# Splitting of weights moved from GpSimd to VectorE, every second cast of attention weights moved to ScalarE, sums of token tiles moved to VectorE

## The chip, the cores and the metric

The kernel runs on one core of a Trainium2 chip. The metric is the device time of one execution in microseconds; of several runs the median is taken. Engines are named as in the profile: PE (TensorE), DVE (VectorE), ACT (ScalarE), POOL (GpSimd), and SP, whose queue issues most DMAs.

## What is computed

An attention without softmax, followed by two MLPs on its 6016 tokens (two batches of 3008):

```python
# u, v: (2, 3008, 256); z: (2, 3008, 64); w_in: (256, 2048); w_out: (2048, 256)
attn = np.maximum((z @ z.T) / 3008, 0.0) ** 2      # per batch
x = (u * (attn @ v)).reshape(6016, 256)
h = x @ w1_in;  x = np.maximum(0.01 * h, h) @ w1_out
h = x @ w2_in;  x = (s * np.maximum(h, 0.0) ** 2 + b) @ w2_out
```

## The kernel before

All matrix products run on operands that are split in two: `hi` is the value cast to the matmul's type (fp32r), `lo` is the value minus `hi`. A product is then three matmuls: hi x hi, hi x lo, lo x hi. Wherever the text says "split" it means one cast for `hi` and one subtraction for `lo`.

**Attention** runs over 12 tiles of queries (512 wide; 448 for the last of each batch), and within a tile over 12 units (`UA`) of two key blocks, 144 units or steps in all. In a unit `scores` (L296) makes four matmuls (L303) into a PSUM tile `f`, ACT applies Relu (L306) and Square (L307) into `a`, DVE casts `hi` (L308) and subtracts `lo` (L314; for the last unit of a tile, L310 and L312). `queue_values` (L317) queues 12 matmuls (L329; 10 in the last unit of a tile) which PE takes two units later, behind the scores of that unit. The first of them reads `hi`, the second `lo`. Every engine works through its own instructions in the order in which the program issues them.

**Weights.** While attention runs, the MLPs' weights, which arrive as 64-bit numbers, are narrowed to 32 bits, split, and written to DRAM. There are 32 items of 512 columns: for each MLP `m`, four groups `g`, kinds `in` and `out`, two halves `h`. An item starts every third step (`s0`), except around the change of batch. `narrow` (L138) spreads its pieces over steps: three on DVE at s0, s0+1, s0+2 (L149; L154, L157; L162, L165), the last of which is followed by `join` on POOL (L178 for `out`; L186 and L190 to L193 for `in`). `halve` (L195) makes the split at s0+5: for `out` items the cast on ACT (L207) and the subtraction on POOL (L208), in the second MLP after a running sum on POOL (L203); for the second half of an `in` item, two casts on ACT (L213) and two subtractions on POOL (L214), for the seven blocks of weights that one step of the MLPs needs. `store` issues the DMAs at s0+8.

Around the change of batch (steps 60 to 74) the keys and values of the second batch are split, with the subtractions on POOL (L116, L252).

**MLPs.** Token tiles are taken in six pairs, and the first product of each MLP is done with seven products of blocks instead of eight (a scheme of Strassen's kind), so each pair needs sums of its token tiles: `pair_sums` (L362) makes four differences T1 to T4 on POOL (L369), and `pair_split` splits them. A pair has eight quads (q = 0 to 7). A quad makes seven products (L395), four sums on DVE from PSUM (L618, L640, L641, L652, L654), activates the previous quad's result on ACT, splits it (`spread`, L586: `hi` on ACT in the first MLP and on DVE in the second, L593; `lo` on DVE, L594) and queues the second product's matmuls (L414), of which PE takes eight after each third of the quad. The sums of the next pair are issued from q = 4 on, one in each third of a quad. At q = 4 of the second pair of the first MLP `bias_columns` (L448) adds two halves on DVE (L449) for a small matmul on PE (L452).

The order of all this is written out by hand: `at(step, fn)` puts a piece of work in front of a unit.

Of the kernel before, what the change touches and what calls it, by code (L numbers as in the profile page):

```python
# [10 lines left out]
F32 = mybir.dt.float32  # L11
F32R = mybir.dt.float32r
# [3 lines left out]
ALU = mybir.AluOpType  # L16
P = 128
# [11 lines left out]
def relu2_attention__then__leaky_mlp__then__relu2_mlp_kernel(  # L29
# [25 lines left out]
    nc = tc.nc  # L55
# [19 lines left out]
    pairs = sorted((ts[i], ts[i + 1]) for ts in by_width.values() for i in range(0, len(ts), 2))  # L75
# [47 lines left out]
    wt_of, staged = {}, {}  # L123
# [14 lines left out]
    def narrow(item):  # L138

        words = raws[item].rearrange("p (n w) -> p n w", w=2)
        low, high = words[:, :, 0], words[:, :, 1]
        w = single.tile([P, 2 * D], F32, tag="w", name="w_single", bufs=4)
        bits = w.bitcast(I32)

        def one():
            nc.vector.tensor_scalar(  # L149
                out=low, in0=low.bitcast(U32), scalar1=2.0 ** -29, scalar2=None, op0=ALU.mult  # L150
            )

        def two():
            nc.vector.tensor_scalar(  # L154
                out=bits, in0=high, scalar1=0x7FFFFFFF, scalar2=None, op0=ALU.bitwise_and
            )
            nc.vector.tensor_scalar(  # L157
                out=w, in0=w, scalar1=HIGH_MAX, scalar2=HIGH_MIN, op0=ALU.min, op1=ALU.max
            )

        def three():
            nc.vector.tensor_scalar(  # L162
                out=bits, in0=bits, scalar1=3, scalar2=0x3FFFFFFF, op0=ALU.logical_shift_left, op1=ALU.bitwise_and
            )
            nc.vector.scalar_tensor_tensor(  # L165
                out=bits, in0=high, scalar=-(1 << 30), in1=bits, op0=ALU.bitwise_and, op1=ALU.bitwise_or
            )
            join(item, w, low)

        return [(0, one), (1, two), (2, three), (5, lambda: halve(item, w)), (8, lambda: store(item))]  # L170

    def join(item, w, low):
        m, g, kind, h = item
# [19 lines left out]
        add(out=a[S4], in0=a[A12], in1=a[S2], op=ALU.subtract)  # L193

    def halve(item, w):  # L195
        m, g, kind, h = item
        add = nc.gpsimd.tensor_tensor
        if kind == "out":
            if m == 2:
                if g == 0 and h == 0:  # L200
                    nc.gpsimd.tensor_copy(out=wsum, in_=w)
                else:
                    add(out=wsum, in0=wsum, in1=w, op=ALU.add)  # L203
            if h == 0:
                staged[m, g, kind] = [outw.tile([P, 2, 2, 2 * D], F32R, tag="outw", name="stage_o")]
            t = staged[m, g, kind][0]
            nc.scalar.copy(out=t[:, h, 0, :], in_=w)  # L207
            add(out=t[:, h, 1, :], in0=w, in1=t[:, h, 0, :].bitcast(F32), op=ALU.subtract)  # L208
        elif h == 1:
            wt = wt_of.pop((m, g))  # L210
            staged[m, g, kind] = [outw.tile([P, 2, 7, P], F32R, tag="outw", name="stage_i") for _ in range(2)]
            for q, t in enumerate(staged[m, g, kind]):
                nc.scalar.copy(out=t[:, 0], in_=wt[:, q, 0:7, :])  # L213
                add(out=t[:, 1], in0=wt[:, q, 0:7, :], in1=t[:, 0].bitcast(F32), op=ALU.subtract)  # L214

    def store(item):
        m, g, kind, h = item
# [78 lines left out]
    def scores(t, p):  # L296
        bb, c, n = tiles[t]
        f = ps_f.tile([P, 2, QT], F32, tag="f", name="f")
        for j in range(2):
            kb = 2 * p + j  # L300
            lhsT = zk[bb, kb // 4][:, (kb % 4) * P:(kb % 4 + 1) * P]
            for h in range(2):
                nc.tensor.matmul(f[:, j, :n], lhsT=lhsT, rhs=zq[t][:, h, :n], start=h == 0, stop=h == 1)  # L303
        a = work.tile([P, 2, QT], F32, tag="a", name="a")[:, :, :n]
        hi, lo = split_parts(a, n)
        nc.scalar.activation(out=a, in_=f[:, :, :n], func=AF.Relu, scale=scale)  # L306
        nc.scalar.activation(out=a, in_=a, func=AF.Square)  # L307
        nc.vector.tensor_copy(out=hi, in_=a)  # L308
        if p == UA - 1:
            nc.vector.tensor_sub(out=lo[:, 0], in0=a[:, 0], in1=hi[:, 0].bitcast(F32))  # L310
            h1 = hi[HALF:P, 1]
            nc.vector.tensor_sub(out=h1, in0=a[HALF:P, 1], in1=h1.bitcast(F32))  # L312
        else:
            nc.vector.tensor_sub(out=lo, in0=a, in1=hi.bitcast(F32))  # L314
        return hi, lo
# [43 lines left out]
            xin[m, t] = xio.tile([P, 2, QT], F32, tag="xin", name="x_in")  # L359
            nc.sync.dma_start(out=xin[m, t][:, :, :n], in_=x_d[m, t][:, :, :n])  # L360

    def pair_sums(m, pr):  # L362

        n = tiles[pr[0]][2]
        (b11, b21), (b12, b22) = ([xin[m, t][:, k, :n] for k in range(2)] for t in pr)
        new = {k: tpool.tile([P, QT], F32, tag="tsum", name="tsum", bufs=4)[:, :n] for k in ("T1", "T2", "T3", "T4")}

        def sub(out, x, y):
            return lambda: nc.gpsimd.tensor_tensor(out=out, in0=x, in1=y, op=ALU.subtract)  # L369

        tsum[m, pr] = {**new, "B11": b11, "B21": b21, "B22": b22}
        return [
            sub(new["T1"], b12, b11), sub(new["T2"], b22, new["T1"]),
            sub(new["T3"], b22, b12), sub(new["T4"], b21, new["T2"]),
        ]
# [81 lines left out]
    def at(step, fn):  # L457
        hooks.setdefault(max(step, 0), []).append(fn)

    with tc.manual_schedule():  # L460
# [61 lines left out]
        for item, s0 in zip(items, places):  # L522
# [2 lines left out]
                    at(s0 + later, piece)  # L525
            at(s0 - 5, lambda item=item: load_w(item))
            hooks.setdefault(s0, []).insert(0, go)
        done = places[len(items) - 1] + 9
        assert done < n_att - 12

        def open_pairs():
# [3 lines left out]
        at(done, open_pairs)  # L535
        at(done + 1, lambda: load_pair(1, pairs[0]))
        sums = []
        at(done + 5, lambda: sums.extend(pair_sums(1, pairs[0])))
        for i in range(4):
            at(done + 5 + i, lambda: sums.pop(0)())  # L540
        for i, name in enumerate(ORDER):
# [61 lines left out]
        for m, pr, q in quads:  # L603
            n = tiles[pr[0]][2]
            k = pair_of.index((m, pr))
            ahead = pair_of[k + 1] if k + 1 < len(pair_of) else None
            x = [ps_x.tile([P, QT], F32, tag="x", name=f"x{i}") for i in range(3)]
            x1, x2, x3 = (y[:, :n] for y in x)
            w = work.tile([P, 2, QT], F32, tag="a", name="a")
            s1, u2 = (w[:, i, :n] for i in range(2))  # L610
            cs = [cpool.tile([P, 2, QT], F32, tag="c", name="c")[:, :, :n] for _ in range(2)]
            c11, c21, c12, c22 = cs[0][:, 0], cs[0][:, 1], cs[1][:, 0], cs[1][:, 1]

            product(x[0], m, pr, q, A11, "B11", True)
            nc.scalar.copy(out=s1, in_=x1)  # L615
            product(x[1], m, pr, q, S2, "T2", True)
            product(x[2], m, pr, q, S1, "T1", True)
            nc.vector.tensor_tensor(out=u2, in0=x2, in1=s1, op=ALU.add)  # L618

            if q == 0 and k:  # L620
                pair_split(m, pr, ORDER[5:7], nc.vector)
            if q == 1 and ahead:
                load_pair(*ahead)
            if q == 6 and ahead:
                pair_split(*ahead, ORDER[0:2], nc.vector)
            if q == NQ - 1 and ahead:
                pair_split(*ahead, ORDER[2:3], nc.vector)
            activate(0)
            if before and before[0] == 1:
                activate(1)  # L630
            if q == 4 and ahead:
                sums.extend(pair_sums(*ahead))
            if sums:
                sums.pop(0)()
            step_chunk()

            product(x[0], m, pr, q, A12, "B21", False)
            act_of(m, c11, x1)
            product(x[1], m, pr, q, S3, "T3", False)
            nc.vector.tensor_tensor(out=c22, in0=x2, in1=s1, op=ALU.add)  # L640
            nc.vector.tensor_tensor(out=c22, in0=x3, in1=c22, op=ALU.add)  # L641
            spread(0)
            if before and before[0] == 2:
                activate(1)
            if q == NQ - 1 and ahead:
                pair_split(*ahead, ORDER[3:4], nc.vector)
            if sums:
                sums.pop(0)()
            step_chunk()

            product(x[1], m, pr, q, A22, "T4", False)
            nc.vector.tensor_tensor(out=c21, in0=x2, in1=s1, op=ALU.add)  # L652
            product(x[2], m, pr, q, S4, "B22", False)
            nc.vector.tensor_tensor(out=c12, in0=x3, in1=u2, op=ALU.add)  # L654
            spread(1)
            if q == NQ - 1 and ahead:
                pair_split(*ahead, ORDER[4:5], nc.vector)
            if sums:
                sums.pop(0)()
            if m == 1 and pr == pairs[-1]:  # L660
                fetch_in(2, q)
            step_chunk()
            before = (m, pr, q, cs)
            if m == 1 and pr == pairs[1] and q == 4:
                bias_columns()
# [40 lines left out]
```

## Time and profile before

| | |
|---|---|
| time, three runs | 1541.13, 1545.22, 1546.81 us; median 1545.22 |
| the profiled execution | 1542.53 us; its span 1540.8 us |
| busy: PE | 1508.7 us (98%) |
| busy: DVE | 1151.4 us (75%); in the first third 90% or more of most slices |
| busy: ACT | 843.7 us (55%) |
| busy: POOL | 333.5 us (22%), mostly in the first third |
| mean granted clock of PE | 0.996 |

Attention takes the first 545 us, the first MLP until about 1027, the second the rest. Busy shares are averages over these stages. Since PE works nearly all the time, its short waits, and what ends them, carry the reading.

### The profile page before, as it was taken

To read this page: it belongs to the slowest core of one execution; us is meant where nothing else is said; L and a number is where in the kernel's file an instruction comes from. 1 tells how busy PE (TensorE), PEld (TensorE's weight loads), DVE (VectorE), ACT (ScalarE), POOL (GpSimd) and SP (SyncE) were. 2 spreads that over 40 slices of the span, in tenths; PEclk is the share of its full clock that TensorE was granted. 3 is DMA by queue.
4 is the path that set the end of the run, shared out by engine and by line. 5 is a ranking of instruction groups with operands and counts; after the bars stand their busy time and mean duration, and the time that the engine had idled before them with its cause. 6 is when DMAs were issued, how large, how long until landed. Compare 5 with 4: busy or idle time off the path is not lost.

```text
span 1540.8 us, 17008 instructions
## 1 busy us (share of the span) xinstructions
PE 1508.7 (98%) x6604; PEld 1239.7 (80%) x6604; DVE 1151.4 (75%) x1365; ACT 843.7 (55%) x1046; POOL 333.5 (22%) x212
## 2 busy tenths in 40 slices
PE   8999999999999999999999999999999999999998
PEld 6877778777787888888889888887877778877786
DVE  7999987999998756656565656566776777676766
ACT  6656666665665644545454546454545545454543
POOL 0344546456654410101010100110010101010000
PEclk9999999999999999999999999999999999999999
DMA  5243433432345430101010101341010101010000
GB/s 156 90 142 110 152 136 115 136 130 84 135 151 217 151 133 1 55 1 51 1 55 1 52 1 65 137 154 55 1 56 1 52 1 55 0 52 1 28 0 28
DMA packets 38834, 113.25 MB, mean 74 GB/s; under 512 B 4064, under 2 KB 13792, under 8 KB 36704
## 3 DMA queue, kind: packets, MB, share of 16 engines
q1 hardware_dynamic: 38528, 111.88, 21.2%
q8 instruction: 52, 0.85, 0.2%
q10 hardware_dynamic: 160, 0.26, 0.1%
q14 instruction: 30, 0.25, 0.1%
q0 software_dynamic: 64, 0.00, 0.0%
HBM read 70.58 MB, written 41.55 MB: 73 GB/s over the span
## 4 chain that ended last, share of the span: by engine, by line
PE 82%; DVE 12%; issue 4%; ACT 1%; DMA 0%; SPq 0%; DVEq 0%
PE acc L414 33%; PE x L395 29%; PE acc L329 16%; PE f L303 5%; DVE lo L314 3%; DVE hi L308 3%; DVE w_single L162 1%; DVE lo L594 1%; DVE hi L312 1%; ACT a L307 1%; ACT a L306 1%; DVE w_single L154 1%; DVE lo L310 1%; DMA raw_v<-in_v_dram 0%; DVE raw_w L149 0%
## 5 line engine op out<-in xcount | busy, mean ns | idle before, releaser
L395 PE MATMUL x<-top,stat_i 128*128 128x512 f32 (+1 forms) x2016 | 498.6, 386 | 0.8 <-DVE c L640 0.8
L414 PE MATMUL acc<-hi,stat_o 128*128 128x512 f32 (+1 forms) x1536 | 483.8, 386 | 0.0
L395 PEld LDWEIGHTS x<-top,stat_i 128*128 128x128 f32 x2016 | 378.2, 188 | 74.4 <-DVE c L640 1.2
L329 PE MATMUL acc<-hi,stat_v 128*128 128x512 f32 (+1 forms) x1152 | 377.2, 392 | 0.4 <-DVE hi L312 0.4
L414 PEld LDWEIGHTS acc<-hi,stat_o 128*128 128x128 f32 x1536 | 288.4, 188 | 54.0 <-DVE hi L593 0.5
L414 PE MATMUL acc<-lo,stat_o 128*128 128x512 f32 (+1 forms) x768 | 302.1, 393 | 3.7 <-DVE lo L594 3.6
L329 PEld LDWEIGHTS acc<-hi,stat_v 128*128 128x128 f32 x1152 | 219.1, 190 | 45.1 <-DVE hi L308 2.1
L306 ACT ACTIVATE a<-f 128x1024 f32<-128x1024 f32 (+1 forms) x144 | 145.5, 1011 | 185.2 <-PE f L303 150.6
L640 DVE TENSOR_TENSOR c<-x,a 128x512 f32<-128x512 f32 (+1 forms) x96 | 65.3, 681 | 234.7 <-PE x L395 234.7
L594 DVE TENSOR_TENSOR lo<-c,hi 128x1024 fp32r<-128x1024 f32 (+1 forms) x192 | 237.9, 1239 | 3.3
L329 PE MATMUL acc<-lo,stat_v 128*128 128x512 f32 (+1 forms) x552 | 217.2, 393 | 14.3 <-DVE lo L314 14.3
L615 ACT COPY a<-x 128x512 f32<-128x512 f32 (+1 forms) x96 | 55.6, 579 | 312.7 <-PE x L395 312.7
L314 DVE TENSOR_TENSOR lo<-a,hi 128x1024 fp32r<-128x1024 f32 (+1 forms) x132 | 209.9, 1590 | 4.6
L369 POOL TENSOR_TENSOR tsum<-x_in 128x512 f32<-128x512 f32 (+1 forms) x24 | 39.5, 1644 | 772.2 <-DMA x_in<-x_d 685.4
L414 PEld LDWEIGHTS acc<-lo,stat_o 128*128 128x128 f32 x768 | 144.1, 188 | 49.5 <-DVE lo L594 23.6
L303 PE MATMUL f<-zq,zk 128*128 128x512 f32 (+1 forms) x576 | 157.0, 395 | 7.2 <-DVE zk L252 5.4
L307 ACT ACTIVATE a<-a 128x1024 f32<-128x1024 f32 (+1 forms) x144 | 150.4, 1044 | 4.6
L308 DVE CAST hi<-a 128x1024 fp32r<-128x1024 f32 (+1 forms) x144 | 117.0, 813 | 39.4 <-ACT a L307 38.8
L329 PEld LDWEIGHTS acc<-lo,stat_v 128*128 128x128 f32 x552 | 105.0, 190 | 40.2 <-DVE lo L314 20.0
L303 PEld LDWEIGHTS f<-zq,zk 128*128 128x128 f32 x576 | 109.9, 191 | 31.4 <-ACT zq L265 5.4
L618 DVE TENSOR_TENSOR a<-x,a 128x512 f32<-128x512 f32 (+1 forms) x96 | 65.2, 680 | 73.7 <-PE x L395 72.9
L584 ACT ACTIVATE c<-c 128x1024 f32<-128x1024 f32 (+1 forms) x96 | 100.3, 1045 | 3.1
(62 smaller groups left out, 1229.9 us busy)
## 6 DMA issues: line engine op xcount, KB each, us to landing
in_d<-stage_i SPq DMA_DIRECT2D x16, 896.0 KB, 8.0
stat_i<-in_d SPq DMA_DIRECT2D x16, 896.0 KB, 4.8
x_in<-x_d SPq DMA_DIRECT2D x20, 512.0 KB, 4.6
raw_w<-in_w_in_dram SPq DMA_DIRECT2D x16, 512.0 KB, 4.6
raw_w<-in_w_out_dram SPq DMA_DIRECT2D x16, 512.0 KB, 4.4
out_d<-stage_o SPq DMA_DIRECT2D x8, 1024.0 KB, 6.4
stat_o<-out_d SPq DMA_DIRECT2D x8, 1024.0 KB, 6.5
raw_v<-in_v_dram SPq DMA_DIRECT2D x14, 384.0 KB, 3.7
```

The lines of the kernel that those rows point to most:

```text
L303: nc.tensor.matmul(f[:, j, :n], lhsT=lhsT, rhs=zq[t][:, h, :n], start=h == 0, stop=h == 1)
L306: nc.scalar.activation(out=a, in_=f[:, :, :n], func=AF.Relu, scale=scale)
L307: nc.scalar.activation(out=a, in_=a, func=AF.Square)
L308: nc.vector.tensor_copy(out=hi, in_=a)
L314: nc.vector.tensor_sub(out=lo, in0=a, in1=hi.bitcast(F32))
L329: nc.tensor.matmul(acc_t[t][dh][:, :n], lhsT=w[:, wh, o:o + P], rhs=x[:, blk % 2, :n], start=blk == 0 and i == 0, stop=half and i == n_i - 1,)
L395: nc.tensor.matmul(x[:, :n], lhsT=w[:, wh, left, :], rhs=r[:, xh, :n], start=first and i == 0, stop=i == 2, skip_group_check=not first,)
L414: nc.tensor.matmul(acc[dh][:, :n], lhsT=w[:, q % 2, wh, o:o + P], rhs=x[:, f, :n], start=q == 0 and f == 0 and i == 0, stop=last,)
L584: nc.scalar.activation(out=c, in_=c, func=AF.Square)
L594: nc.vector.tensor_sub(out=lo, in0=c, in1=hi.bitcast(F32))
L618: nc.vector.tensor_tensor(out=u2, in0=x2, in1=s1, op=ALU.add)
L640: nc.vector.tensor_tensor(out=c22, in0=x2, in1=s1, op=ALU.add)
```

## The change

In `narrow`, `halve` becomes a list of pieces that stand at steps of their own: for `out` items the cast on ACT at s0+4 and the subtraction at s0+5; for the second half of `in` items the first cast at s0+6, the first subtraction and the second cast at s0+7, the second subtraction at s0+8. The subtractions go from POOL to DVE. The running sum of L203 stays on POOL. `store` moves from s0+8 to s0+10, and what comes after the last item moves one step. In `scores`, the cast of `hi` goes from DVE to ACT in units with odd `p`. In the MLPs `pair_sums` issues on DVE; the first pair's sums, which run during attention, stay on POOL.

```diff
@@ narrow
-        return [(0, one), (1, two), (2, three), (5, lambda: halve(item, w)), (8, lambda: store(item))]
+        return [
+            (0, one), (1, two), (2, three),
+            *(((4 if item[2] == "out" else 6) + i, fn) for i, fn in enumerate(halve(item, w))),
+            (10, lambda: store(item)),
+        ]
@@ halve
+        if kind == "in" and h == 0:
+            return []
+
+        def hi_out():
             if m == 2:
                 if g == 0 and h == 0:
                     nc.gpsimd.tensor_copy(out=wsum, in_=w)
                 else:
-                    add(out=wsum, in0=wsum, in1=w, op=ALU.add)
+                    nc.gpsimd.tensor_tensor(out=wsum, in0=wsum, in1=w, op=ALU.add)
             if h == 0:
                 staged[m, g, kind] = [outw.tile([P, 2, 2, 2 * D], F32R, tag="outw", name="stage_o")]
+            nc.scalar.copy(out=staged[m, g, kind][0][:, h, 0, :], in_=w)
+
+        def lo_out():
             t = staged[m, g, kind][0]
-            nc.scalar.copy(out=t[:, h, 0, :], in_=w)
-            add(out=t[:, h, 1, :], in0=w, in1=t[:, h, 0, :].bitcast(F32), op=ALU.subtract)
-        elif h == 1:
-            wt = wt_of.pop((m, g))
-            staged[m, g, kind] = [outw.tile([P, 2, 7, P], F32R, tag="outw", name="stage_i") for _ in range(2)]
-            for q, t in enumerate(staged[m, g, kind]):
-                nc.scalar.copy(out=t[:, 0], in_=wt[:, q, 0:7, :])
-                add(out=t[:, 1], in0=wt[:, q, 0:7, :], in1=t[:, 0].bitcast(F32), op=ALU.subtract)
+            nc.vector.tensor_tensor(out=t[:, h, 1, :], in0=w, in1=t[:, h, 0, :].bitcast(F32), op=ALU.subtract)
+
+        def hi_in(q):
+            t = outw.tile([P, 2, 7, P], F32R, tag="outw", name="stage_i")
+            staged.setdefault((m, g, kind), []).append(t)
+            nc.scalar.copy(out=t[:, 0], in_=wt_of[m, g][:, q, 0:7, :])
+
+        def lo_in(q):
+            t = staged[m, g, kind][q]
+            nc.vector.tensor_tensor(
+                out=t[:, 1], in0=wt_of[m, g][:, q, 0:7, :], in1=t[:, 0].bitcast(F32), op=ALU.subtract
+            )
+            if q == 1:
+                wt_of.pop((m, g))
+
+        if kind == "out":
+            return [hi_out, lo_out]
+        return [lambda: hi_in(0), lambda: (lo_in(0), hi_in(1)), lambda: lo_in(1)]
@@ scores
-        nc.vector.tensor_copy(out=hi, in_=a)
+        (nc.scalar.copy if p % 2 else nc.vector.tensor_copy)(out=hi, in_=a)
@@ pair_sums
-            return lambda: nc.gpsimd.tensor_tensor(out=out, in0=x, in1=y, op=ALU.subtract)
+            return lambda: eng.tensor_tensor(out=out, in0=x, in1=y, op=ALU.subtract)
@@ before attention
-        done = places[len(items) - 1] + 9
+        done = places[len(items) - 1] + 10
-        at(done + 5, lambda: sums.extend(pair_sums(1, pairs[0])))
+        at(done + 5, lambda: sums.extend(pair_sums(1, pairs[0], nc.gpsimd)))
@@ the quads
-                sums.extend(pair_sums(*ahead))
+                sums.extend(pair_sums(*ahead, nc.vector))
```

## Rows read from the trace of the kernel before

**Rows 1.** Order of time, PE: score matmuls opening units 3, 12, 60, 84, 132 (start, us).
```profile
18.28 1.09 PE L303 MATMUL f<-zq,zk 128*128 128x512 f32 x4
...
51.22 1.09 PE L303 MATMUL f<-zq,zk 128*128 128x512 f32 x4
...
232.10 0.97 PE L303 MATMUL f<-zq,zk 128*128 128x448 f32 x4
...
317.64 1.09 PE L303 MATMUL f<-zq,zk 128*128 128x512 f32 x4
...
505.43 0.97 PE L303 MATMUL f<-zq,zk 128*128 128x448 f32 x4
```

**Rows 2.** Waits, whole run: who waited for whom, us in total, times, longest.
```profile
PEld acc L414 <- DVE lo L594: 23.6, 53, 2.0
...
PEld acc L329 <- DVE lo L314: 20.0, 16, 2.0
...
PEld f L452 <- DVE wtot L449: 0.9, 1, 0.9
```

**Rows 3.** Order of time, POOL and DVE around the stall at unit 20.
```profile
73.67 5.34 POOL L214 TENSOR_TENSOR stage_i<-wt,stage_i 128x896 fp32r<-128x896 f32 x2 [1.06 <-ACT stage_i L213]
...
74.67 2.36 DVE L162 TENSOR_SCALAR w_single<-w_single 128x512 int32<-128x512 int32 x1
```

**Rows 4.** Lines L162, L165, L308, L178, L203: count, then shortest, median, longest in ns.
```profile
L162 DVE TENSOR_SCALAR w_single<-w_single x32: 411/421/2361, 53.0 to 476.8; 128x512 int32<-128x512 int32 x32
...
L165 DVE SCALAR_TENSOR_TENSOR w_single<-raw_w,w_single x32: 691/693/2499, 53.5 to 477.2; 128x512 int32<-128x512 int32 x32
...
L308 DVE CAST hi<-a x144: 612/686/2272, 12.2 to 544.7; 128x1024 fp32r<-128x1024 f32 x120, 128x896 fp32r<-128x896 f32 x24
...
L178 POOL TENSOR_TENSOR w_single<-w_single,raw_w x16: 1666/1689/1702, 79.6 to 478.0; 128x512 int32<-128x512 int32 x16
...
L203 POOL TENSOR_TENSOR wsum<-wsum,w_single x7: 2142/2157/2160, 337.3 to 479.8; 128x512 f32<-128x512 f32 x7
```

**Rows 5.** Busy by stretch: PE, PEld, DVE, ACT, POOL, then PEclk, DMA share, GB/s.
```profile
328.00:331.00 3.00, 3.00 (x8) 2.35 (x8) 2.96 (x5) 2.40 (x3) 0.68 (x2) 0.50 0.00 0
```

**Rows 6.** Groups by line and shape: busy us, mean ns, idle time before them.
```profile
L640 DVE TENSOR_TENSOR c<-x,a 128x512 f32<-128x512 f32 x80 | 55.3, 692 | 199.7 <-PE x L395 199.7
...
L594 DVE TENSOR_TENSOR lo<-c,hi 128x896 fp32r<-128x896 f32 x32 | 35.8, 1118 | 0.5
...
L388 DVE TENSOR_TENSOR top<-tsum,top 128x512 fp32r<-128x512 f32 x36 | 24.7, 685 | 5.2 <-ACT top L387 5.2
...
L593 ACT CAST hi<-c 128x1024 fp32r<-128x1024 f32 x80 | 80.5, 1046 | 0.0
...
L213 ACT CAST stage_i<-wt 128x896 fp32r<-128x896 f32 x16 | 14.3, 945 | 4.9 <-POOL wt L193 4.9
```

**Rows 7.** Order of time: scores, Relu and Square of unit 87.
```profile
331.98 1.09 PE L303 MATMUL f<-zq,zk 128*128 128x512 f32 x4
...
333.11 1.03 ACT L306 ACTIVATE a<-f 128x1024 f32<-128x1024 f32 x1 [2.68 <-PE f L303]
...
334.17 1.06 ACT L307 ACTIVATE a<-a 128x1024 f32<-128x1024 f32 x1
```

**Rows 8.** Order of time, second MLP: start of a quad, the second `lo`.
```profile
1227.42 0.84 PE L395 MATMUL x<-top,stat_i 128*128 128x512 f32 x3
...
1227.48 1.23 DVE L594 TENSOR_TENSOR lo<-c,hi 128x1024 fp32r<-128x1024 f32 x1
```

**Rows 9.** Waits, 240 to 300 us: PE's weight loads at the change of batch.
```profile
PEld acc L329 <- DVE lo L314: 3.2, 6, 1.1
```

**Rows 10.** Order of time, second MLP: a sum on POOL, a wait of PE.
```profile
1373.24 1.31 POOL L369 TENSOR_TENSOR tsum<-x_in 128x512 f32<-128x512 f32 x1 [69.07 <-DMA x_in<-x_d]
...
1377.36 0.19 PEld L414 LDWEIGHTS acc<-lo,stat_o 128*128 128x128 f32 x1 [2.02 <-DVE lo L594]
```

**Rows 11.** Waits, 1389 to 1400 us: a quad of the second MLP without sums.
```profile
PEld acc L414 <- DVE lo L594: 0.4, 1, 0.4
```

More of the change, by code (lines that the diff above doesn't have):

```diff
@@ L196, in halve @@
         m, g, kind, h = item
-        add = nc.gpsimd.tensor_tensor
-        if kind == "out":
+        if kind == "in" and h == 0:
+            return []
+        def hi_out():
             if m == 2:
@@ L360, in load_pair, with pair_sums @@
             nc.sync.dma_start(out=xin[m, t][:, :, :n], in_=x_d[m, t][:, :, :n])
-    def pair_sums(m, pr):
+    def pair_sums(m, pr, eng):
         n = tiles[pr[0]][2]
```

## The prediction

> **What bounds the kernel now.** Read the page's busy shares first: PE is busy nearly the whole span, DVE far less but most of all in the first third, so what can be won is what PE still loses. How much that is shows in PE's own order of time, at the score matmuls (L303) that open each attention unit. From unit 3 to unit 12 nine units take 51.22 - 18.28 = 32.94 us, 3.66 us each, without any stall [rows 1]. A unit has 16 matmuls, so one is 0.229 us; the last unit of a tile has 14. A stall-free tile of 12 units is 12 x 3.66 - 0.46 = 43.46 us, four are 173.8. The four tiles from 51.22 took 180.9, a loss of 7.0 us; the four from 317.64 took 187.8, a loss of 13.9 [rows 1]. These are the eight tiles during which weights are prepared.
>
> Next the view of waits: PE's weight loads wait 20.0 us in 16 waits for L314, the `lo` of the attention weights, and 23.6 us in 53 waits for L594, its counterpart in the MLPs [rows 2]. So PE stops when DVE delivers a `lo` late. Why it is late shows in the order of time around one stall. L214, the two `lo` of summed weights, holds POOL from 73.67 to 79.01; DVE's L162 inside that stretch takes 2.36 us [rows 3], while its shortest takes 0.41 and its median is 0.42 [rows 4]. DVE and POOL do not run such instructions side by side: the later one waits. The `lo` behind them on DVE comes late and PE stops at unit 20. The same pattern stands at all eight tiles, in step with L214, which runs once in each. After three of the four stalls of the second batch the granted clock is 0.50 (the 1.2 GHz level instead of 2.4) for 3 us or more, one of them in [rows 5]: 1.5 us or more each, inside the 13.9.
>
> The Trainium skill (SBUF — State Buffer, Who interferes with whom) says that VectorE and GpSimd share a port pair as an exclusive lock that is held for the whole instruction, and that a VectorE operation with two SBUF inputs competes for it too. The 2.36 us above agrees. The rule also speaks against this change, since it adds DVE instructions of that kind; the first rival is that case.
>
> **The change, part by part.**
> (a) L214 and L208 leave POOL, 16 instructions each; their work goes to DVE. Nearest rows: 1.12 us for 128x896 and 0.69 us for 128x512 [rows 6]. Per tile two of each: 2 x 1.12 + 2 x 0.69 = 3.6 us, or 0.3 us per unit. What goes: the long lock of two L214 in a row, and with it the stalls of 7.0 + 13.9 = 20.9 us.
> (b) The `hi` cast of odd units goes from DVE (median 0.69 us [rows 4]) to ACT, where the same cast in the first MLP takes 1.05 [rows 6]. DVE gains 0.34 us per unit, so (a) and (b) about cancel in its time. ACT gains 0.52 per unit. In [rows 7] the scores start at 331.98 and ACT's square ends at 335.23, 3.25 later; an ACT cast of 1.05 and a `lo` of 1.23 [rows 8] bring `lo` to 5.6 us after the start, with hand-overs. PE takes it two units later, behind the next-but-one scores and one matmul: 2 x 3.66 + 0.92 + 0.23 = 8.5. The cover is 2.9 us; today it is 3.1. Nothing is paid as long as that holds. At the batch change (240 to 300 us) POOL splits v and z, which stays; PE waits there 3.2 us for `lo` [rows 9], and DVE's casts are stretched up to 2.27 us [rows 4]. With every second cast off DVE I take 2.0 of the 3.2 as won; the ends are 0 and 3.2.
> (c) The pieces are spread: `out` weights at 4 and 5 units after their start, `in` at 6, 7 and 8, stores at 10 instead of 8. The new DVE instructions wait for an ACT cast one unit earlier; that cast stands in front of the unit's own activations on ACT's queue, so it is done a unit before. The stores on SP's queue move behind them by two units; nothing reads the buffers before the first MLP, and the write-out of a tile lies inside the 12 units until its slot is needed again. No cost. What is new is one heavy step, 8 units after the second `in` item: `lo` of `in` 1.12, `lo` of `out` 0.69, L162 0.42, L165 0.69 [rows 4] and the unit's `lo` 1.23, together 4.15 us (its `hi` is on ACT). The step before has the other `lo` of `in`, two narrowing instructions taken like L162, a `hi` and a `lo`: 3.9. Against 2 x 3.66 that is a backlog of 0.7 us. The POOL instructions that stay there, L178 at 1.69 and in the second half L203 at 2.16 [rows 4], can each hold a DVE instruction for at most their own length: up to 3.85 more, so 0.7 to 4.6 against a cover of about 3. A stall is 0 to 1.6 us per tile, bounds of 0 to 13 for eight tiles; only the last four have L203. Taken: 0.4 in each of those, 1.5.
> (d) The sums of token tiles: 44 POOL instructions of the MLPs go to DVE at 0.69 [rows 6], three in the fifth quad of a pair (q = 4), one in the next. Won: the locks. From 1373.24 on POOL makes sums, and in that stretch PE's load waits 2.02 for a `lo` [rows 10]. Without sums a quad of the second MLP waits 0.4 [rows 11]; 48 x 0.4 = 19.2 of the 23.6 are that, which stays, so 4.4 us go. Cover for the new ones: DVE idles before L640 for 199.7 / 80 = 2.5 us each time [rows 6], which takes the first and the fourth. The second delays the second `lo` by 0.69; that `lo` ends at 1228.71, 1.3 us into the next quad (which begins at 1227.42 [rows 8]), and PE wants it after nine products and five queued matmuls, 14 x 0.23 = 3.2 us into it. The third falls behind that `lo`. So nothing is paid, except once: at the second pair of the first MLP L449 (the bias column) now queues behind the second and third sum, and PE, which waits for L449 at the end of that quad [rows 2], waits 2 x 0.69 = 1.4 longer. Bounds: 0, if L449 had time left, to 2.9, if the clock fell as in [rows 5].
>
> **The sum.** 20.9 + 2.0 - 1.5 + 4.4 - 1.4 = 24.4 us. The profiled execution took 1542.5 (span 1540.8): 1518.1. It lay 2.7 under the median of the runs shown, so the forecast for the median is 1521.
>
> **The rivals.**
> *The locks go on, smaller.* The heavy step of (c) meets L178 and L203, and the four tiles of the second batch keep their stalls and their drops of the clock: 13.9 of the 24.4 stay, 1535. For it: L162 shows that one POOL instruction can cost DVE its whole length. Against: none that stays comes as two long ones in a row, and the backlog needs over 3 us.
> *The change does not do what it says:* L214 only marks the place, the stall comes of L165, L178 and the load of a tile's last unit, and the added DVE work takes what the lock gives. Only (d) is left: 1542. Against: the stall of [rows 3] lies six units or more into a tile, that ahead of [rows 5] three units behind a border; what they share is L214.
> *Slower: ACT becomes the late engine.* An odd unit asks 1.03 + 1.06 [rows 7] + 1.05 = 3.14 us of ACT; with a weight cast of 0.95 [rows 6] it is 4.1, over the pitch of 3.66. It decides once ACT falls back by more than the 2.9 us of cover; then each odd unit adds its excess of about 0.5 us to the path: 72 x 0.5 = 36, less 24.4: 1557. Against: the even unit needs 2.1 (3.0 with a cast), so two units ask at most 7.1 of 7.3. The Trainium skill (ScalarE: Activation LUTs, Rules for kernel authors) tells one to use VectorE rather than ScalarE for simple elementwise work; the 1.05 against 0.69 above agrees, and moving 72 casts costs the two engines 26 us more in all by it, which counts only where ACT is late.
>
> **How the numbers follow.** Forecast 0.77, locks go on 0.12, not as it says 0.07, slower 0.04. Lower end: all 3.2 of the batch change and no new stall: 20.9 + 3.2 + 4.4 = 28.5, 1517; the runs of before scatter by 2 to 4 us around their median: 1514. Upper end: nothing at the batch change and three quarters of the bound of (c), 1.2 of new stall in each of eight tiles: 20.9 - 9.6 + 3.0 = 14.3, 1531. A difference of 0.5% is about what a measurement of this kernel can tell from none, 7.7 us: under 1537.5 is faster. Forecast and most of the second case lie there: 0.88; 0.08 same; 0.04 slower.
>
> **What would show it.** Right: tiles of 43.5 us in the starts of the score matmuls in both batches; waits of PE for L314 under 8 us in all; no stretch of half clock inside attention; L162 at 0.42 throughout most of its 32; the wait for L449 grown by over a microsecond; waits for L594 near 20. Wrong: PE waiting for `lo` at units 86 to 88 of each tile of the second batch (first rival), at units 20, 32, 44 as before (second), or the ACT cast standing before most waits of PE in odd units (third).

## The result, and the profile after

The changed kernel takes 1515.4 us (median of five runs, 1514.4 to 1517.8) against 1543.7 us for the kernel before on the same chip (1541.1 to 1546.8): the ratio is 0.9815, 95% interval 0.9805 to 0.9826. The gain is 28.3 us; 24.4 were forecast, and 1521 us. The profiled execution took 1514.4 us with a span of 1512.4.

Lines have moved by 20 from `scores` on: L303, L308, L314 and L329 are now L323, L328, L334 and L349; L369, L414, L449, L594 and L640 are L389, L434, L469, L614 and L660. L208 and L214 became L217 and L226 on DVE, L178 is L182, L203 is L210.

The starts of the score matmuls, for the same units as in [rows 1] but unit 3 (start, duration in us):

```profile
51.00 1.09 PE L323 MATMUL f<-zq,zk 128*128 128x512 f32 x4
...
224.87 0.97 PE L323 MATMUL f<-zq,zk 128*128 128x448 f32 x4
...
307.97 1.09 PE L323 MATMUL f<-zq,zk 128*128 128x512 f32 x4
...
481.84 0.97 PE L323 MATMUL f<-zq,zk 128*128 128x448 f32 x4
```

Four tiles from 51.00 take 173.87 us, four from 307.97 take 173.87: the 173.8 of a stall-free PE. The 20.9 us that the eight tiles lost are gone. The stretch between (units 60 to 83) takes 83.1 us where [rows 1] give 85.5, 2.4 less.

PE's waits over the whole run, to be held against [rows 2]:

```profile
PEld acc L434 <- DVE lo L614: 18.7, 49, 0.6
...
PEld f L472 <- DVE wtot L469: 1.9, 1, 1.9
...
PEld acc L349 <- DVE lo L334: 1.8, 3, 1.0
```

The wait for the attention's `lo` fell from 20.0 us to 1.8. That for the MLPs' `lo` lost its long ones (longest 0.6, before 2.0) and kept 49 short ones. The wait for the bias column grew from 0.9 to 1.9. L162, which stood at up to 2.36 us [rows 4], is never held now, and in this execution the granted clock does not fall within attention:

```profile
L162 DVE TENSOR_SCALAR w_single<-w_single x32: 413/420/428, 53.1 to 454.0; 128x512 int32<-128x512 int32 x32
```
```profile
327.00:331.00 4.00, 4.00 (x19) 3.30 (x18) 3.93 (x5) 3.87 (x5) 1.40 (x2) 1.00 0.72 210
```

(The second row is a stretch as in [rows 5]: the granted clock is the 1.00 near its end.)

The two spans differ by 28.3 us (1540.75 and 1512.43). Where they are, by PE's instructions: start of the kernel 0.2, the eight tiles 20.9, the change of batch 2.4, the second MLP 4.1 (508.7 to 504.7 us, from its first product to the end of its last matmul); the first MLP takes 0.4 more (0.7 won where POOL's sums ran, 1.1 lost at the bias column); the rest, 1.1, lies behind the last matmul, where 5.1 us became 4.1.

The heavy step that the prediction named, DVE and POOL in order of time, units 87 and 88:

```profile
322.00 1.08 DVE L226 TENSOR_TENSOR stage_i<-wt,stage_i 128x896 fp32r<-128x896 f32 x1
323.00 0.68 DVE L217 TENSOR_TENSOR stage_o<-w_single,stage_o 128x512 fp32r<-128x512 f32 x1
...
324.66 1.22 DVE L334 TENSOR_TENSOR lo<-a,hi 128x1024 fp32r<-128x1024 f32 x1
325.80 1.53 DVE L149 TENSOR_SCALAR raw_w<-raw_w 128x512 int32<-128x512 uint32 x1
327.25 1.78 DVE L328 CAST hi<-a 128x1024 fp32r<-128x1024 f32 x1
329.06 1.23 DVE L334 TENSOR_TENSOR lo<-a,hi 128x1024 fp32r<-128x1024 f32 x1
```
```profile
324.82 2.21 POOL L182 TENSOR_TENSOR w_single<-w_single,raw_w 128x512 int32<-128x512 int32 x1 [10.16 <-DVE w_single L165]
327.12 1.36 POOL L210 TENSOR_TENSOR wsum<-wsum,w_single 128x512 f32<-128x512 f32 x1
```
```profile
330.64 0.39 PE L349 MATMUL acc<-lo,stat_v 128*128 128x512 f32 x1
```

Its five instructions run from 322.00 to 325.88. Behind them L182 holds L149, and L210 holds the cast of unit 88, 1.1 us each, as the prediction's upper bound supposed. The `lo` of unit 88 ends at 330.29 and PE takes it at 330.64: of the cover of about 3 us, 0.35 is left. No stall, but with so little left it is the narrowest place of the eight tiles; the same place shows 0.34 in each of the next two tiles and 0.81 in the last.

### The profile page after: what moved, and what is told of

Same layout as the page of the kernel before. It is cut to its first block, busy times and chain, and to the rows that moved or that the text cites. A ratio compares the mean times of both kernels' runs of the same rounds, so it can differ in the third digit from the quotient of the medians.

```text
span 1512.4 us, 16921 instructions
## 1 busy us (share of the span) xinstructions
PE 1498.3 (99%) x6604; PEld 1237.7 (82%) x6604; DVE 1089.8 (72%) x1369; ACT 915.8 (61%) x1118; POOL 191.8 (13%) x136
## 4 chain that ended last, share of the span: by engine, by line
PE 97%; DVE 2%; DMA 0%; ACT 0%; issue 0%; SPq 0%; DVEq 0%
PE acc L434 34%; PE x L415 30%; PE acc L349 25%; PE f L323 8%; DMA raw_v<-in_v_dram 0%; DVE lo L614 0%; DVE lo L334 0%; DVE c L660 0%; DVE hi L332 0%; DVE c L661 0%; ACT a L327 0%; ACT a L326 0%; DVE hi L613 0%; DVE hi L328 0%; SPq L261 0%
## 5 line engine op out<-in xcount | busy, mean ns | idle before, releaser
L434 PE MATMUL acc<-hi,stat_o 128*128 128x512 f32 (+1 forms) x1536 | 483.7, 386 | 0.0
L349 PE MATMUL acc<-hi,stat_v 128*128 128x512 f32 (+1 forms) x1152 | 373.1, 388 | 0.0
L434 PEld LDWEIGHTS acc<-hi,stat_o 128*128 128x128 f32 x1536 | 288.4, 188 | 53.7
L434 PE MATMUL acc<-lo,stat_o 128*128 128x512 f32 (+1 forms) x768 | 301.7, 393 | 0.2
L349 PEld LDWEIGHTS acc<-hi,stat_v 128*128 128x128 f32 x1152 | 217.1, 188 | 42.4 <-DVE hi L328 0.5
L614 DVE TENSOR_TENSOR lo<-c,hi 128x1024 fp32r<-128x1024 f32 (+1 forms) x192 | 230.0, 1198 | 3.3
L334 DVE TENSOR_TENSOR lo<-a,hi 128x1024 fp32r<-128x1024 f32 (+1 forms) x132 | 188.8, 1431 | 56.5 <-ACT hi L328 54.0
L660 DVE TENSOR_TENSOR c<-x,a 128x512 f32<-128x512 f32 (+1 forms) x96 | 65.3, 680 | 221.4 <-PE x L415 221.4
L349 PE MATMUL acc<-lo,stat_v 128*128 128x512 f32 (+1 forms) x552 | 213.8, 387 | 0.7 <-DVE lo L334 0.7
L434 PEld LDWEIGHTS acc<-lo,stat_o 128*128 128x128 f32 x768 | 144.1, 188 | 44.7 <-DVE lo L614 18.7
L323 PE MATMUL f<-zq,zk 128*128 128x512 f32 (+1 forms) x576 | 156.7, 394 | 7.0 <-DVE zk L272 5.3
L323 PEld LDWEIGHTS f<-zq,zk 128*128 128x128 f32 x576 | 109.5, 191 | 31.0 <-ACT zq L285 5.3
L349 PEld LDWEIGHTS acc<-lo,stat_v 128*128 128x128 f32 x552 | 104.0, 188 | 22.0 <-DVE lo L334 1.8
L638 DVE TENSOR_TENSOR a<-x,a 128x512 f32<-128x512 f32 (+1 forms) x96 | 65.2, 679 | 68.6 <-PE x L415 67.8
L604 ACT ACTIVATE c<-c 128x1024 f32<-128x1024 f32 (+1 forms) x96 | 100.3, 1045 | 3.0
L613 ACT CAST hi<-c 128x1024 fp32r<-128x1024 f32 (+1 forms) x96 | 94.9, 1027 | 0.0
L593 ACT ACTIVATE c<-c 128x512 f32<-128x512 f32 (+1 forms) x96 | 79.7, 830 | 1.9 <-DVE c L672 1.9
```

The source lines that it names most:

```text
L349: nc.tensor.matmul(acc_t[t][dh][:, :n], lhsT=w[:, wh, o:o + P], rhs=x[:, blk % 2, :n], start=blk == 0 and i == 0, stop=half and i == n_i - 1,)
L434: nc.tensor.matmul(acc[dh][:, :n], lhsT=w[:, q % 2, wh, o:o + P], rhs=x[:, f, :n], start=q == 0 and f == 0 and i == 0, stop=last,)
L593: nc.scalar.activation(out=out, in_=x, func=AF.Relu)
L604: nc.scalar.activation(out=c, in_=c, func=AF.Square)
L613: (nc.scalar.copy if m == 1 else nc.vector.tensor_copy)(out=hi, in_=c)
L614: nc.vector.tensor_sub(out=lo, in0=c, in1=hi.bitcast(F32))
```

## The experiments

The theory that was put to the test is that L214 on POOL makes the eight stalls by holding DVE; the rivals, that DVE's load makes them, or that L214 only marks their place. Below, "tiles" is what the eight tiles with weights take beyond 173.8 us per four, first batch + second batch: 7.0 + 13.9 before, 0 + 0 in the changed kernel.

**L214 left out.** In the kernel before:

```diff
-                add(out=t[:, 1], in0=wt[:, q, 0:7, :], in1=t[:, 0].bitcast(F32), op=ALU.subtract)
@@ store: the hi part in the place of lo too
-            nc.sync.dma_start(out=in_d[m, 2 * g + q], in_=t...)
+            for part in range(2):
+                nc.sync.dma_start(out=in_d[m, 2 * g + q][:, part * 7 * P:(part + 1) * 7 * P], in_=t[:, 0]...)
```

> The kernel before without L214: the subtractions of the in weights are left out, and the hi part is stored in the place of lo too (two DMAs of half the size instead of one); nothing else is moved. Theory (L214 on POOL makes the eight stalls): no wait at any of the eight tiles, each 43.5 us; the change of batch and the MLPs as before: 20.9 us less, 1522 to 1525 us. Rival (L214 only marks the place, the pieces at five units after the start come too close together): at least half of the stalls stay, 1533 us or more.

Measured: 1524.9 us, ratio 0.9877 (0.9861 to 0.9894), 18.9 us less. Tiles 0.0 + 0.4, by the starts of the same units as above; change of batch as before. These starts, and the waits of PE:

```profile
52.64 1.09 PE L306 MATMUL f<-zq,zk 128*128 128x512 f32 x4
...
226.50 0.97 PE L306 MATMUL f<-zq,zk 128*128 128x448 f32 x4
...
312.07 1.09 PE L306 MATMUL f<-zq,zk 128*128 128x512 f32 x4
...
486.28 0.97 PE L306 MATMUL f<-zq,zk 128*128 128x448 f32 x4
```
```profile
PEld acc L332 <- DVE lo L317: 4.7, 9, 1.1
```

(L306 and L317 are L303 and L314 there; seven of the nine waits lie at the start of attention and around the change of batch, and the other two, in the second batch, are 0.4 and 0.2 us.) With nothing else moved, the stalls are gone. L214 is the cause and not a mark of the place.

**The three parts one at a time.** First the weights' `lo` on DVE at the new steps, with `hi` and the sums as before:

```diff
@@ the changed kernel
-        (nc.scalar.copy if p % 2 else nc.vector.tensor_copy)(out=hi, in_=a)
+        nc.vector.tensor_copy(out=hi, in_=a)
-                sums.extend(pair_sums(*ahead, nc.vector))
+                sums.extend(pair_sums(*ahead, nc.gpsimd))
```

> The kernel before with the first part of the change alone: lo of the MLP weights on DVE in pieces at their new steps; the hi cast of attention stays on DVE in every unit, the sums of token tiles stay on POOL. Theory (the lock of L214 on POOL makes the eight stalls): the eight tiles take 43.5 us each, 20.9 us less in all; the heavy step, 8 units after the second in item, now has a hi of 0.69 us more on DVE and the cover left there in the changed kernel is 0.34 us, so some 0.5 us at units 86 to 88 of four tiles, 2 us; the change of batch and the MLPs stay: 1525 us. Rival (DVE's load makes lo late, and only the casts taken off DVE help): DVE gets 28 us more work, so 1544 us or slower, with the stalls at units 20, 32, 44, 56 still there.

Measured: 1527.4 us, ratio 0.9885 (0.9871 to 0.9900). Tiles 0.0 + 5.0, the change of batch as before:

```profile
PEld acc L349 <- DVE lo L334: 9.6, 11, 1.6
```

The eight stalls went although DVE got more work, against the rival. New ones of 0.7 to 1.4 us came just behind the heavy step (units 87 and 88) in the second batch, 5.0 us where 2 were expected.

Then the cast alone, in the kernel before:

```diff
-        nc.vector.tensor_copy(out=hi, in_=a)
+        (nc.scalar.copy if p % 2 else nc.vector.tensor_copy)(out=hi, in_=a)
```

> The kernel before with the second part alone: the hi cast of odd units on ACT; lo of weights and sums stay on POOL. Theory (lock): L214 still holds L162 and L165 for over 2 us each; each lo behind them comes 0.7 us earlier, so a stall of about 1 us is left at each of the eight tiles, without the fall of the clock; the change of batch gains 2.5 us: 1528 us, L162 still at 2.3 us where L214 runs. Rival (load): the stalls go as in the changed kernel, 1520 us.

Measured: 1537.0 us, ratio 0.9946 (0.9931 to 0.9961). Tiles 5.3 + 7.8, the change of batch 2.4 us shorter. L162 is still held:

```profile
PEld acc L329 <- DVE lo L314: 15.9, 11, 2.1
```
```profile
L162 DVE TENSOR_SCALAR w_single<-w_single x32: 414/428/2360, 54.6 to 467.3; 128x512 int32<-128x512 int32 x32
```

The stalls are 1.3 to 2.0 us instead of 1.4 to 3.8, and the granted clock stays at 1.00 behind them; they stay at the same units. Theory, with more left than the 1 us each that was expected. The total is 9 us slower than expected: 5 of that are these tiles, most of the rest the second MLP, to which the result of the third part speaks.

Then the sums alone, in the kernel before:

```diff
-                sums.extend(pair_sums(*ahead))
+                sums.extend(pair_sums(*ahead, nc.vector))
```

> The kernel before with the third part alone: the sums of token tiles on DVE. Theory: attention as before; the five quads of the MLPs in which POOL's sums hold DVE give 4.8 us back, the bias column costs 1.1 us: 3.7 us less, 1540 us. Rival (DVE in the second MLP has no room for the sums): its quads q = 4 and 5 grow, nothing won or slower, 1544 to 1550 us.

Measured: 1539.6 us, ratio 0.9963 (0.9950 to 0.9976): 5.8 us less. The waits in the second MLP have no long ones left:

```profile
PEld acc L414 <- DVE lo L594: 18.5, 48, 0.6
```

The second MLP takes 504.8 us in this trace. With the sums on POOL it took 508.7 in the profiled execution of before, 511.7 and 514.4 in the two runs above, 511.1 without L214 and 510.1 in the run with new steps alone, below. So the price of POOL's sums is not one number: 4 to 10 us, from trace to trace, though the program of the MLPs is the same in these five. With the sums on DVE the second MLP takes 504.7 to 504.9 us in all six traces of kernels with the changed kernel's MLPs. The reason can be seen at the third pair of the second MLP. POOL, with nothing else to do, starts on the sums in the pair's second quad already (q = 1). Before, the first sum starts 8.4 us into that quad, which begins at 1206.38, and costs nearly nothing. In the run with the weights' `lo` alone it starts 6.6 us into the same quad, and PE waits 1.9 us:

```profile
1189.94 2.20 PE L415 MATMUL x<-top,stat_i 128*128 128x512 f32 x9
```
```profile
1196.50 1.15 POOL L389 TENSOR_TENSOR tsum<-x_in 128x448 f32<-128x448 f32 x1 [78.24 <-DMA x_in<-x_d]
```
```profile
PEld acc L434 <- DVE lo L614: 1.9, 1, 1.9
```

POOL starts when the token tiles' DMA lands, at no fixed place of the quad, and holds whichever DVE instruction it meets. On DVE the sums have a fixed place.

**Back to POOL, at the new steps.** The changed kernel with the `in` subtractions on POOL again:

```diff
-            nc.vector.tensor_tensor(
+            nc.gpsimd.tensor_tensor(
                 out=t[:, 1], in0=wt_of[m, g][:, q, 0:7, :], in1=t[:, 0].bitcast(F32), op=ALU.subtract
```

> The changed kernel with the subtractions of in weights back on POOL, but at their new steps, one unit apart. Theory (it is two long instructions on POOL in a row that hold DVE twice within one unit): each of them alone is covered, 1515 to 1518 us. Rival (any such instruction on POOL makes its stall): a wait for lo at each of the eight tiles of 1 to 2 us, 1525 to 1535 us.

Measured: 1515.9 us, ratio to before 0.9814 (0.9797 to 0.9830). Tiles 0.0 + 0.6.

```profile
L226 POOL TENSOR_TENSOR stage_i<-wt,stage_i 128x896 fp32r<-128x896 f32 x16 | 47.6, 2977 | 0.0
```
```profile
PEld acc L349 <- DVE lo L334: 2.8, 6, 1.0
```

The instructions hold POOL for 3.0 us each, longer than before (2.6), and PE hardly waits. That these subtractions run on POOL is not what costs, as long as the rest of the change stands, the `out` subtractions on DVE included.

**Together again, but on DVE.** The changed kernel with all pieces at one step:

```diff
-            *(((4 if item[2] == "out" else 6) + i, fn) for i, fn in enumerate(halve(item, w))),
-            (10, lambda: store(item)),
+            *((5, fn) for fn in halve(item, w)),
+            (8, lambda: store(item)),
```

> The changed kernel without the new steps: all pieces of a half stand at five units after the start, stores at eight, subtractions on DVE as in the changed kernel. Theory now, after the run with the subtractions on POOL at the new steps cost nothing (what counts is that no two long holds of DVE fall into one unit): DVE meets both subtractions at once and stands in its order behind two ACT casts of 0.93 us that come after POOL's last sum; 2 x 1.08 of work and up to 1.9 of waiting in one unit, against a cover of 2.9: a stall of 0.5 to 1.5 us at each of eight tiles, 1520 to 1527 us. Rival (leaving POOL is what counts): 1515 us as the changed kernel.

Measured: 1517.5 us, ratio to before 0.9829 (0.9814 to 0.9843). Tiles 0.0 + 1.4: a stall of 0.35 us in each tile of the second batch, less than expected. Two in a row ask 2 x 1.08 us of DVE in one unit, and with every second cast on ACT the cover takes all but this.

**The new steps alone.** The kernel before with the pieces at their new steps, subtractions on POOL, casts on DVE, sums on POOL:

```diff
@@ the changed kernel
-            nc.vector.tensor_tensor(out=t[:, h, 1, :], ...)
+            nc.gpsimd.tensor_tensor(out=t[:, h, 1, :], ...)
@@ and the three lines of the runs above (in weights, hi, sums) as before
```

> The kernel before with the pieces at their new steps alone: subtractions stay on POOL, casts of hi on DVE, sums on POOL. Theory (the two long holds in one unit make the stalls): the eight stalls of 1.4 to 3.8 us go or shrink to under 1 us, also without the clock's fall; with hi on DVE in every unit there is less cover, so some 0.5 to 1 us each at units 86 to 89 is left: 1526 to 1530 us. Rival (the work must leave POOL unless hi leaves DVE): 1538 us or more.

Measured: 1539.8 us, ratio 0.9973 (0.9963 to 0.9984), only 4.1 us less. Tiles 5.7 + 11.9: the stalls of before are gone from their units, and others came one to four units later, in seven of the eight tiles.

```profile
PEld acc L349 <- DVE lo L334: 24.4, 28, 2.2
```
```profile
322.33 3.11 POOL L226 TENSOR_TENSOR stage_i<-wt,stage_i 128x896 fp32r<-128x896 f32 x1
323.37 2.35 DVE L149 TENSOR_SCALAR raw_w<-raw_w 128x512 int32<-128x512 uint32 x1
...
326.15 2.57 POOL L226 TENSOR_TENSOR stage_i<-wt,stage_i 128x896 fp32r<-128x896 f32 x1
326.77 3.03 DVE L334 TENSOR_TENSOR lo<-a,hi 128x1024 fp32r<-128x1024 f32 x1
...
329.86 0.19 PEld L349 LDWEIGHTS acc<-lo,stat_v 128*128 128x128 f32 x1 [1.49 <-DVE lo L334]
```

Each POOL instruction still holds one of DVE's (L149 at 2.35, where its shortest takes 0.41; `lo` at 3.03 instead of 1.23), and with every cast on DVE the two units do not make it up. So the theory of the two long holds in one unit falls too.

What fits the runs so far is a balance: per unit DVE has a cover of about 3 us; its own work, its waits for POOL and the pieces that fall into neighbouring units all draw on it, and PE stalls by what they draw beyond it. This is put together from the runs, and none was made to test it alone. But the traces show the cover being used up. From the end of a `lo` to the matmul that reads it there are 3.24 us in an undisturbed unit of the kernel before and 2.88 in an odd one of the changed kernel. In units 109 to 112, around the heavy step, the changed kernel has 2.44, 1.24, 1.10 and 0.34 left. With the same pieces and every cast on DVE, 1.86, 0.66 and 0.06 are left in units 109 to 111, and PE stalls for 1.4. With the `in` subtractions back on POOL, unit 21 keeps 0.39 instead of 1.32: DVE is held, but the cover pays for it.

With two of the three reliefs (subtractions off POOL, apart, every second cast off DVE) 0.6 to 5.0 us are left in the tiles; in the run with 0.6 only the `in` subtractions went back, so what the `out` ones carry was not separated. The cast alone leaves 13.1, the new steps alone 17.5. The move off POOL alone, with all pieces at one step and every cast on DVE, was not run.

**All casts on ACT.** The rival on the slower side, pushed twice as far:

```diff
-        (nc.scalar.copy if p % 2 else nc.vector.tensor_copy)(out=hi, in_=a)
+        nc.scalar.copy(out=hi, in_=a)
```

> The changed kernel with the hi cast of every unit on ACT. The slower rival of the prediction asks when ACT becomes the late engine. Over a tile with weights ACT then has 12 x 3.14 + 0.6 + 2 x 0.62 + 2 x 0.93 = 41.4 us of 43.5; in the 448-wide tile ahead of the change of batch 12 x 2.82 + 8 x 0.83 + 0.6 = 41.1 of 39.0 us. Theory (cover of 2.9 us, ACT late only there): as the changed kernel in the weight tiles, 1 to 3 us lost around the change of batch, 1515 to 1518 us. Rival (ACT's chain is already near its limit): waits of PE for lo in many units, 1530 us or more.

Measured: 1515.2 us, ratio to before 0.9816 (0.9802 to 0.9831), as the changed kernel. Tiles 0 + 0, the change of batch another 0.6 us shorter.

```profile
PEld acc L349 <- DVE lo L334: 1.0, 1, 1.0
```

ACT is not the late engine, even there, and the 1 to 3 us put down for it did not come. The count of 41.1 us against 39.0 was too high: the trace has ACT busy for 37.2 us of the 39.6 of that tile. In a tile with weights it is busy for up to 40.8 of 43.5 us, so this run goes close to ACT's limit and not beyond it.

**What the prediction took as a fixture.** Each quad of the second MLP waits 0.4 us for `lo` [rows 11], also in the changed kernel. ACT has finished the square (L604) that the first cast reads well before DVE's wait ahead of L660 ends; only DVE's order puts two sums from PSUM in front of it. In the second trace of the changed kernel:

```profile
1110.99 0.68 DVE L638 TENSOR_TENSOR a<-x,a 128x512 f32<-128x512 f32 x1
...
1111.12 1.06 ACT L604 ACTIVATE c<-c 128x1024 f32<-128x1024 f32 x1
...
1114.55 0.69 DVE L660 TENSOR_TENSOR c<-x,a 128x512 f32<-128x512 f32 x1 [2.88 <-PE x L415]
```

The square ends at 1112.18, 0.5 us after DVE, done with L638, fell idle (the expectation below has it done by then), and DVE stands idle for another 2.4 us. Three runs were made: the changed kernel once more on the same chip, then with `spread(0)` of the second MLP moved ahead of the products of the second third, then with the bias column's sum at the beginning of its quad as well:

> The changed kernel itself, on the chip of the next two, for comparison: 1515 us; its quads of the second MLP take 10.47 us as in the kernel before, and the fifth quad of the second pair of the first MLP 12.42.

```diff
@@ the quads, behind the first step_chunk()
+            if before and before[0] == 2:
+                spread(0)
@@ behind L661
-            spread(0)
+            if before and before[0] == 1:
+                spread(0)
```

> The changed kernel with the first spread of a quad in the second MLP (hi and lo on DVE) issued ahead of the products of the second third, so ahead of L660 and L661 in DVE's order; it reads what ACT finished before DVE falls idle there. Theory (the wait of 0.4 us for lo in each quad, which the prediction left as a fixture, is DVE's order alone: two sums from PSUM stand ahead of hi and lo): quads of 10.20 instead of 10.47 us, 48 x 0.27 = 13 us less, 1502 us, no wait left of the 18.7 us for L614. Rival (lo waits for ACT's square, or the sums it passes then come late for PE): 1515 us or slower, with waits of PE for L660.

```diff
@@ bias_columns
-        nc.vector.tensor_tensor(out=wtot, in0=wsum[:, 0:D], in1=wsum[:, D:2 * D], op=ALU.add)
@@ the quads, ahead of the first product
+            if m == 1 and pr == pairs[1] and q == 4:
+                nc.vector.tensor_tensor(out=wtot, in0=wsum[:, 0:D], in1=wsum[:, D:2 * D], op=ALU.add)
```

> The same, and the sum for the bias column (L469) issued at the beginning of its quad instead of at its end, behind the sums of token tiles. Theory (the 1.1 us that the change added there, and the 1.1 that the kernel before lost, are DVE's queue ahead of that sum): the fifth quad of the second pair falls from 12.42 to some 10.4 us, 2 us below early_lo: 1500 us. Rival (PE waits there for something else): as early_lo.

Measured: 1515.2, 1504.8 and 1503.1 us; the ratios to before are 0.9810 (0.9796 to 0.9823), 0.9743 (0.9730 to 0.9756) and 0.9729 (0.9716 to 0.9742). DVE's order of time in the run with the first move (left: start and duration), where cast and `lo` now stand ahead of the two sums (here L662, L663; the first is shown):

```profile
1109.49 0.69 DVE L638 TENSOR_TENSOR a<-x,a 128x512 f32<-128x512 f32 x1 [0.73 <-PE x L415]
1110.97 0.69 DVE L613 CAST hi<-c 128x1024 fp32r<-128x1024 f32 x1 [0.78 <-ACT c L604]
1111.69 1.22 DVE L614 TENSOR_TENSOR lo<-c,hi 128x1024 fp32r<-128x1024 f32 x1
1113.30 0.69 DVE L662 TENSOR_TENSOR c<-x,a 128x512 f32<-128x512 f32 x1 [0.38 <-PE x L415]
```

and PE's waits in that run for the MLPs' `lo` (18.7 us before the move) and for L662:

```profile
PEld acc L434 <- DVE lo L614: 0.4, 1, 0.4
...
PEld x L415 <- DVE c L662: 2.9, 6, 1.2
```

Most quads fall from 10.47 to 10.20 us, as expected; the last quad of the first five pairs keeps its time. There the rival came true: PE waits 0.3 to 0.4 us for L662, which now stands behind the cast and `lo` (five of the six waits; that of 1.2 lies at the start of the first MLP, and the changed kernel has it too). The second MLP takes 493.8 us instead of 504.9, 11.0 less, where 13 were expected; these quads are most of the difference. The second move takes the quad with the bias column from 12.42 to 10.64 us. Together they make the fastest kernel of this study, 41 us below the one before.

## Why the prediction was right, step by step

The time (1515.4) lies in the range, 6 us below the forecast. Of these, 1.6 are the median of the kernel before, taken as 1545.2 from three runs and 1543.7 over five; the rest are the terms below. Direction and main mechanism, the hold of L214 on DVE, stood the test.

(a) The 20.9 us of the eight tiles were won to the tenth, and L214 is their cause (1524.9 us without it). But the step as written, "with it the stalls", gave the whole to the move off POOL. That is not so: the move and the new steps without the casts leave 5.0 us, and with the rest in place the `in` subtractions can go back to POOL for 0.6. The loss had one cause; its cure has three parts, each of which, as the runs suggest, buys some of the same cover.

(b) "(a) and (b) about cancel in its time" is right as a sum and wrong as a price: the cast was worth 2.4 us at the change of batch, where 2.0 was taken, and 5.0 at the tiles beside the other parts (7.8 by itself), where nothing was put down. ACT's cover held, also with twice the casts.

(c) The heavy step was found in the right place and its size is right (4.15 forecast, 3.88 measured, POOL's holds 2.2 of at most 3.85). The 1.5 us taken for it did not come: cover of 0.35 us was left. In the run without the casts on ACT it did come, with 5.0.

(d) is the term that was mis-sized. 4.4 us was read off one execution. In the pair of traces the sums gave 4.7 (0.66 and 4.06), but over five traces with POOL's sums the second MLP takes 508.7 to 514.4, a mean of 511.2, against 504.8 with DVE's: 6.4. The trace of before was the cheapest of the five. The bias column's new wait was forecast at 1.4 and is 1.1.

The sum, 24.4, comes out 3.9 under the 28.3 of the two spans: 1.5 for the stall that did not come, 0.4 at the change of batch, 0.3 each for the sums and the bias column, and 0.2 at the start and 1.1 behind the last matmul; the last tenth is rounding. The last two were named by no step, and the change is not shown to be their cause: unit 12 starts between 51.0 and 52.7 us over all traces, and the run with the casts alone, with POOL's sums, also ends 4.1 us behind its last matmul. They may be the scatter of single executions.

The rivals: the locks did not go on as stalls, though they go on as holds (L149 and the cast of unit 88 above). That L214 only marks the place fell with the run without it; that the added DVE work takes back what the move gives is true of 5.0 of the 20.9 us as long as no cast goes to ACT. ACT did not become the late engine, even with all casts on it.

The Trainium skill's rule on the shared port pair (SBUF — State Buffer, Who interferes with whom) carried the reading of (a) and of the sums; the holds above agree with it: L162 at 2.36 us beside L214 [rows 3], 0.42 without.

## What to carry to other kernels

Where PE waits for one engine, count that engine's cover per step (from the input's arrival to the moment PE needs the result), and enter into it the engine's own work, the holds by a neighbour and the pieces from other steps; a stall is what exceeds it, so one relief can look worthless alone and decide in company. Work on POOL that starts when a DMA lands holds DVE at a place that changes from run to run: its price has to be read over several traces, and moving it to a fixed place in DVE's order takes away the scatter too. A short wait that is repeated in every step and is called structure deserves a look at the order of the waiting engine's queue first.

## What was not expected of the hardware

Stalls of the same length did not always bring the clock down. [rows 5] follow two waits of PE at unit 86, 0.4 us for `hi` and 2.0 for `lo`, behind which the granted clock stood at the 1.2 GHz level for 3.4 us. The same two waits at unit 122 were followed by no fall, nor were the single waits of 2.0 us at units 32, 44 and 56 of the first batch. In the run with the casts alone, two of the waits behind POOL's sums in the second MLP brought it down as well (3.4 us each), again a wait for `hi` and then 2.0 us for `lo`. At the start of attention, behind the first waits, it stood at that level for 6.8 us in the second trace of the changed kernel and not at all in the first. What decides stays open.
